# Two tiles' attention blocks side by side on TensorE in a fused window-attention and MoE kernel

## The chip, the cores and the metric

One NeuronCore of a Trainium2 chip runs the whole kernel as one program. The metric is the time of one execution on the device, in microseconds (us); lower is better. The engines are PE (TensorE, matmuls), PEld (its weight loads), DVE (VectorE), ACT (ScalarE), POOL (GpSimd) and SP (SyncE, which here issues the DMAs).

## What is computed

Window attention over q, k and v (8 batches, 8 heads, 576 positions, head width 64, window 64), then a feed-forward block over the 4608 tokens of width 512: hidden width 1024, a softmax-weighted activation, a layer norm with gain, and an output product.

```python
scores = scale * q @ k.T                       # per head
scores = where(0 <= i - j < 64, scores, -1e9)
attn = softmax(scores);  x = attn @ v          # x: 4608 x 512
h = x @ w_in                                   # 4608 x 1024
solu = h * softmax(h)
ln = (solu - mean) / sqrt(var + 1e-6) * g
y = ln @ w_out                                 # 4608 x 512, float32
```

## The kernel before

The tokens are cut into 36 tiles of 128. Iteration t of the main loop emits, in this order on PE: one tiny matmul for the scale of tile t+1 (`x_scale`); the input product of tile t (`moe_in`, 24 matmuls of 128x128 by 128x512 in f16, three passes for accuracy); the values block of tile t+1 (`values`, 32 matmuls of 128x64 in f32, attention weights times v); the scores block of a tile three or four ahead (`scores` inside `attend`, 32 matmuls of 64x64 in f32); and the output product of tile t-3 (`moe_out`, 24 f16 matmuls). Tiles 0 to 2 use f32 products, and the first eight tiles transpose their attention weights on PE (`transposes`); later tiles write them to DRAM and read them back transposed by DMA (`soft_turn`, lines 646 and 649). The layer-norm result goes the same way (`turn`, lines 819 and 822).

The order is made by a small planner, `Plan`. Every operation is registered with an engine, an estimated cost, and what it reads and writes. On PE the planner keeps the order in which the operations were registered. On DVE, ACT, POOL and SP it runs a list schedule: each time an engine is free, the ready operation with the earliest due time is put next, due times being counted back from PE's work. At run time each engine takes its own list strictly in turn.

Buffers are rings, sized in `RINGS`. The ones that matter here lie in PSUM, 8 banks in all: `pH` (hidden layer, two banks, one place), `pS` (scores, two banks, one place), `t` (two places of one bank: early transposes, the scale matmuls, the last tiles' transposes), `pX` (values) and `pO` (output product), one bank each. In SBUF: `qk` 3 places, `v` 4, `vx` 2, `sS` (softmax) 3, `xH` 2, `raw` 4 (first the raw weights, then attention weights and their transposes).

After the scores, `softmax` runs on DVE (line 593 scales and masks, line 598 takes the maximum), ACT (line 602, eight exponentials) and POOL (line 618, scaling), and `soft_planes` (line 638) splits the halves for the DMA. For tiles in `MASKED` PE adds the mask instead (line 549), DVE reduces straight from PSUM in two halves (line 586) and ACT reads PSUM. After the values, ACT (line 708) and DVE (line 709) scale the result into `xH`. After the input product, `moe_norm` reads `pH` three times: maximum on DVE (line 752), exponential on ACT (line 758), product and sum on DVE (line 761); then the layer norm follows. `planes` makes the f16 halves (lines 810 and 813), `join` gathers the values of two blocks (line 532), and line 887 moves the output product out of `pO`. `HOMES` lists, for the first 13 tiles, tasks that run on another engine than their default.

Of the kernel before, what the change touches and what calls it, by code (L numbers as in the profile page):

```python
# [37 lines left out]

HASTE = 1
# [11 lines left out]
    ("PT", 1, 1): "DVE", ("PT", 2, 0): "DVE", ("PT", 4, 0): "DVE", ("PT", 4, 1): "ACT", ("PT", 5, 1): "ACT",  # L51
    ("PT", 6, 0): "DVE", ("PT", 6, 1): "ACT", ("PT", 7, 0): "DVE", ("high", 0, 0): "POOL", ("high", 1, 0): "DVE",
    ("high", 1, 1): "POOL", ("high", 3, 0): "POOL", ("high", 4, 0): "DVE", ("high", 4, 1): "POOL",
    ("high", 5, 0): "POOL", ("high", 5, 1): "POOL", ("high", 6, 0): "POOL", ("high", 7, 0): "POOL",
    ("high planes", 1, 1): "DVE", ("high planes", 2, 0): "POOL", ("high planes", 2, 1): "POOL",
    ("high planes", 3, 0): "DVE", ("high planes", 3, 1): "DVE", ("high planes", 4, 0): "POOL",
    ("high planes", 4, 1): "POOL", ("high planes", 5, 1): "DVE", ("high planes", 6, 0): "DVE",
    ("high planes", 6, 1): "DVE", ("high planes", 7, 0): "POOL", ("high planes", 7, 1): "DVE",
    ("high planes", 8, 0): "POOL", ("high planes", 8, 1): "DVE", ("high planes", 9, 1): "DVE",
    ("high planes", 10, 0): "POOL", ("high planes", 10, 1): "POOL", ("high planes", 11, 0): "POOL",  # L60
    ("high planes", 11, 1): "POOL", ("join", 0, 1): "ACT", ("join", 1, 0): "DVE", ("join", 1, 1): "DVE",
    ("join", 3, 0): "DVE", ("join", 3, 1): "ACT", ("join", 4, 0): "ACT", ("join", 5, 0): "ACT",
    ("join", 7, 0): "ACT", ("join", 8, 0): "DVE", ("join", 10, 0): "DVE", ("join", 10, 1): "POOL",
    ("join", 11, 1): "DVE", ("join", 12, 0): "DVE", ("join", 12, 1): "DVE", ("low bits", 1, 0): "DVE",
    ("low bits", 4, 0): "DVE", ("norm", 4, 1): "DVE", ("norm", 6, 1): "DVE", ("norm", 7, 1): "DVE",
    ("norm", 8, 1): "DVE", ("norm", 9, 0): "DVE", ("norm", 10, 0): "DVE", ("norm", 10, 1): "DVE",
    ("norm", 11, 0): "DVE", ("norm", 12, 0): "DVE", ("norm", 12, 1): "DVE", ("planes", 3, 0): "POOL",
    ("planes", 4, 0): "POOL", ("planes", 5, 1): "POOL", ("planes", 6, 0): "POOL", ("planes", 6, 1): "POOL",
    ("planes", 7, 1): "POOL", ("planes", 8, 0): "POOL", ("planes", 9, 0): "POOL", ("planes", 9, 1): "POOL",
    ("planes", 10, 1): "POOL", ("planes", 11, 1): "POOL", ("planes", 12, 0): "POOL", ("planes", 12, 1): "POOL",  # L70
    ("scale", 0, 0): "ACT", ("scale", 0, 1): "POOL", ("scale", 1, 0): "ACT", ("scale", 1, 1): "POOL",
    ("scale", 2, 0): "ACT", ("scale", 5, 1): "ACT", ("scale", 8, 1): "DVE", ("scale", 9, 1): "ACT",
    ("scale", 11, 0): "ACT", ("scale", 11, 1): "ACT", ("scale", 12, 1): "DVE", ("soft", 8, 0): "DVE",
    ("soft", 8, 1): "ACT", ("soft", 9, 1): "ACT", ("soft", 10, 0): "DVE", ("soft", 10, 1): "ACT",
    ("soft", 11, 0): "DVE",
# [3 lines left out]
MASKED = (1, 4, 5)  # L79
# [145 lines left out]
def tile_window_attention_solu_moe(  # L225
# [312 lines left out]
    def PS(t):  # L538
        return T("pS", t, [P, 2, NPAIR, P], pool=ps_s)

    def scores(t):
        first = first_of(t)

        def emit():
            q, k = Q(t), K(t)
            if t in MASKED:
                mk = masksB[first]
                for r in range(2):
                    nc.tensor.matmul(
                        PS(t)[:, r], identB,  # L550
                        bass.AP(tensor=mk.tensor, offset=mk.offset, ap=[mk.ap[0], [0, NPAIR], mk.ap[1]]),
                        start=True, stop=False)
            for p in range(NPAIR):
                for half in range(2):
                    for r in range(2):
                        rs = slice(r * D, (r + 1) * D)
                        keys = k[rs, p, :P]
                        if half or first == 0:
# [7 lines left out]
                            PS(t)[half * WIN:(half + 1) * WIN, r, p],  # L566
                            q[rs, p, half * WIN:(half + 1) * WIN], keys, start=t not in MASKED,
                            stop=t not in MASKED or p == NPAIR - 1)

        plan.op("PE", 1430 if t in MASKED else 1000, emit, [("qk", t)], [("pS", t)], loose=t < LOOSE)  # L570

    def softmax(t):
# [4 lines left out]
        if t < HEADS:  # L577
            for h in range(H):
                plan.op("DVE", 370, lambda h=h: nc.vector.tensor_tensor_reduce(
                    SS(t)[:, h], PS(t)[:, h // NPAIR, h % NPAIR], mk, scale=-SCALE, scalar=BIG,  # L580
                    op0=ALU.add, op1=ALU.min, accum_out=cols("nmx", h)),
                    [("pS", t)], [("sS", t, h), ("nmx", t, h)], lat=200)
        elif t in MASKED:
            for r in range(2):
                hs = slice(r * NPAIR, (r + 1) * NPAIR)
                plan.op("DVE", 650, lambda r=r, hs=hs: nc.vector.tensor_reduce(
                    T("nmx", t, [P, H], pool=st)[:, hs], PS(t)[:, r], axis=AX.X, op=ALU.max, negate=True),
# [4 lines left out]
        else:  # L592
            plan.op("DVE", 1230, lambda: nc.vector.scalar_tensor_tensor(  # L593
                SS(t), PS(t).rearrange("q r p n -> q (r p) n"), SCALE,
                bass.AP(tensor=mk.tensor, offset=mk.offset, ap=[mk.ap[0], [0, H], mk.ap[1]]),
                ALU.mult, ALU.add),
                [("pS", t)], [("sS", t, h) for h in range(H)])
# [3 lines left out]
        for h in range(H):  # L601
            plan.op("ACT", 580, lambda h=h: nc.scalar.activation(  # L602
                SS(t)[:, h], PS(t)[:, h // NPAIR, h % NPAIR] if t in MASKED else SS(t)[:, h], AF.Exp,
# [75 lines left out]

    def PX(t):  # L680
        return T("pX", t, [P, NC, P], pool=ps_x)
# [9 lines left out]
    def values(t):  # L691
        def emit():
            for p in range(NPAIR):
# [8 lines left out]
        plan.op("PE", 1100, emit, turned(t)  # L702
                + [("v", t), ("vx", t, 0), ("vx", t, 1)], [("pX", t)],
# [151 lines left out]
    def moe_out(t):  # L855
# [3 lines left out]
        def PO():  # L859
            if last:  # L860
                return T(*bank, [P, NC, P], pool=ps_x).rearrange("p a b -> p (a b)")
# [177 lines left out]
```

## Time and profile before

| what | us |
|---|---|
| median of 3 runs | 508.1 |
| the three runs | 506.03, 509.09, 508.1 |
| the profiled execution | 508.81 |
| its span, first to last instruction | 506.6 |
| PE busy in the span | 492.7 |
| DVE, ACT, POOL busy | 391.7, 334.8, 277.5 |

Busy times are unions of the instructions' times on an engine. Matmuls overlap in the array, so a PE that is always busy still loses time where starts are further apart than within a run of equal matmuls. The granted clock of TensorE was 0.999 of full over the span. Idle time of an engine that nobody waits for costs nothing.

### The profile page before, as it was taken

The numbers are of one execution on the slowest core, as the hardware profiler recorded it, in microseconds if no ns is written. First come the engines' busy times: TensorE is split into PE (matmuls) and PEld (weight loads), VectorE is DVE, ScalarE is ACT, GpSimd is POOL, SyncE is SP. The second block draws the span as 40 slices with busy tenths as digits, with TensorE's granted clock in tenths as the row PEclk, the third lists the DMA queues.
The fourth block names the chain that finished last, engine by engine and source line by source line (L and its number), as shares of the span: only waits on it lengthen the run. The fifth ranks groups of instructions, "written<-read, shape, count | busy, mean of one in ns | idle before, by whom it ended". The sixth has DMA issues, their size and how long they took to land.

```text
span 506.6 us, 11800 instructions
## 1 busy us (share of the span) xinstructions
PE 492.7 (97%) x4297; PEld 265.0 (52%) x4297; DVE 391.7 (77%) x875; ACT 334.8 (66%) x958; POOL 277.5 (55%) x477
## 2 busy tenths in 40 slices
PE   8899999999999999999999999999999999999997
PEld 7665555545445555555555555555455555544453
DVE  3798899988898887777887887887787888855430
ACT  5677776678675665767776776776676776764340
POOL 5716768756545666565555555555555556572110
PEclk9999999999999999999999999999999999999999
DMA  8991324769999999999999999999999998778311
GB/s 344 416 390 39 113 74 130 205 180 228 268 249 273 282 240 261 257 270 243 258 269 295 222 277 280 246 272 222 278 252 246 287 251 203 198 234 188 105 41 43
DMA packets 157450, 115.60 MB, mean 228 GB/s; under 512 B 129872, under 2 KB 130128, under 8 KB 156880
## 3 DMA queue, kind: packets, MB, share of 16 engines
q1 hardware_dynamic: 157392, 114.84, 82.3%
q8 instruction: 34, 0.56, 0.5%
q14 instruction: 24, 0.20, 0.1%
HBM read 41.42 MB, written 41.42 MB: 164 GB/s over the span
## 4 chain that ended last, share of the span: by engine, by line
PE 70%; DMA 9%; DVE 5%; SPq 4%; POOL 3%; ACT 1%; issue 1%; ACTq 0%
PE pO L876 29%; PE pH L737 26%; PE pX L698 6%; PE pS L565 5%; DMA raw<-pd 4%; DMA yT<-yd 3%; SPq L822 2%; PE pH L725 1%; SPq L649 1%; PE pX L876 1%; DMA yd<-pl 1%; POOL w_outH L500 1%; DVE raw L378 1%; DVE mst L752 1%; DVE e L761 1%
## 5 line engine op out<-in xcount | busy, mean ns | idle before, releaser
L876 PE MATMUL pO<-w_outH,yT 128*128 128x512 f16 x544 | 167.7, 380 | 2.7 <-DMA yT<-yd 2.5
L737 PE MATMUL pH<-w_inH,xH 128*128 128x512 f16 x528 | 161.8, 379 | 0.3 <-DVE xH L709 0.3
L618 POOL TENSOR_SCALAR sS<-sS,rec 128x128 f32<-128x128 f32 x252 | 102.4, 425 | 79.3 <-DVE rec L614 60.8
L876 PEld LDWEIGHTS <-yT 128*128 128x128 f16 x840 | 79.6, 98 | 99.6 <-issue 4.7
L737 PEld LDWEIGHTS <-xH 128*128 128x128 f16 x792 | 75.1, 98 | 89.2 <-DVE xH L709 0.8
L602 ACT ACTIVATE sS<-sS,nmx 128x128 f32<-128x128 f32 x264 | 102.3, 391 | 16.5 <-DVE nmx L598 11.1
L876 PE MATMUL pO<-w_outL,yT 128*128 128x512 f16 x272 | 103.1, 379 | 0.0
L737 PE MATMUL pH<-w_inL,xH 128*128 128x512 f16 x264 | 99.0, 379 | 0.0
L782 POOL TENSOR_SCALAR e<-e,mst 128x512 f32<-128x512 f32 x62 | 50.8, 826 | 50.3 <-DVE mst L756 31.6
L752 DVE TENSOR_REDUCE mst<-pH 128x1 f32<-128x1024 f32 x36 | 44.0, 1223 | 34.4 <-PE pH L737 33.3
L887 ACT ACTIVATE ot<-pO,bound 128x512 f32<-128x512 f32 x34 | 23.3, 685 | 57.6 <-PE t_x L469 48.3
L708 ACT ACTIVATE xH<-pX,xscale 128x512 f16<-128x512 f32 x33 | 22.7, 687 | 43.9 <-PE pX L698 43.6
L776 POOL TENSOR_TENSOR mst<-mst,neghalf 128x1 f32<-128x1 f32 x36 | 20.3, 564 | 56.1 <-DVE mst L774 53.4
L638 POOL COPY raw<-sS 128x1024 uint16<-128x1024 uint16 x50 | 50.7, 1040 | 0.2
L602 ACT ACTIVATION_READ_ACCUMULATOR sS<-sS,nmx 128x1 f32 x264 | 50.1, 190 | 0.0
L769 ACT ACTIVATE unread<-e,mst 128x1024 bf16<-128x1024 f32 x36 | 41.0, 1139 | 12.6 <-DVE mst L764 11.2
L758 ACT ACTIVATE e<-pH,mst,xscale 128x1024 f32<-128x1024 f32 x33 | 39.6, 1199 | 11.0 <-DVE mst L756 11.0
L761 DVE CUSTOM_DVE_ANT_0 e<-pH,e 128x1024 f32<-128x1024 f32 x36 | 43.7, 1215 | 2.7 <-ACT e L758 2.6
L813 DVE TENSOR_TENSOR pl<-e,pl 128x512 f16<-128x512 f32 x49 | 39.5, 809 | 2.0 <-ACT pl L810 1.9
L565 PE MATMUL pS<-qk 64*64 64x128 f32 x1152 | 40.6, 280 | 0.0
L598 DVE TENSOR_REDUCE nmx<-sS 128x8 f32<-128x1024 f32 x32 | 38.5, 1202 | 0.0
L593 DVE SCALAR_TENSOR_TENSOR sS<-pS,maskNone 128x1024 f32<-128x1024 f32 x26 | 31.6, 1216 | 3.8 <-PE pS L565 3.7
(131 smaller groups left out, 714.9 us busy)
## 6 DMA issues: line engine op xcount, KB each, us to landing
qk<-qk SPq DMA_DIRECT2D x36, 640.0 KB, 5.1
yd<-pl SPq DMA_DIRECT2D x33, 512.0 KB, 3.4
pd<-raw SPq DMA_DIRECT2D x28, 512.0 KB, 4.0
v<-vS SPq DMA_DIRECT2D x36, 256.0 KB, 3.5
y<-ot SPq DMA_DIRECT2D x35, 256.0 KB, 3.4
raw<-w_in SPq DMA_DIRECT2D x4, 1024.0 KB, 10.6
raw<-w_out SPq DMA_DIRECT2D x4, 1024.0 KB, 9.9
yT<-yd SPq DMA_TRANSPOSE x33, 5.1
```

The costliest lines, as they stand in the source:

```text
L565: nc.tensor.matmul(PS(t)[half * WIN:(half + 1) * WIN, r, p], q[rs, p, half * WIN:(half + 1) * WIN], keys, start=t not in MASKED, stop=t no ...
L602: plan.op("ACT", 580, lambda h=h: nc.scalar.activation(SS(t)[:, h], PS(t)[:, h // NPAIR, h % NPAIR] if t in MASKED else SS(t)[:, h], AF.Ex ...
L618: SS(t)[:, h], SS(t)[:, h], rec()[:, h:h + 1]) if e == "ACT" else units[e].tensor_scalar(
L638: plan.op(e, {"POOL": 1050, "ACT": 1000, "DVE": 700}[e], lambda x=x, e=e: copy_on(e)(PP(t)[:, :, 4 * x:4 * x + 4].rearrange("p k h n -> p ...
L737: plan.op("PE", 218, lambda n=n, c=c, k=k, w=w: nc.tensor.matmul(PH(t)[:, hs], X(t, k)[:, c], w(c, h), start=(n == 0), stop=(n == len(pass ...
L752: plan.op("DVE", 1230, lambda: nc.vector.tensor_reduce(nmax(), PH(t), axis=AX.X, op=ALU.max, negate=True), [("pH", t)], [key(0)])
L758: plan.op("ACT", 1320, lambda: nc.scalar.activation(E(t), PH(t), AF.Exp, bias=nmax(), scale=XS(t, 2) if scaled else 1.0, accum_out=se()), ...
L761: plan.op("DVE", 1310, lambda: nc.vector.tensor_tensor_reduce(E(t), PH(t), E(t), scale=1.0, scalar=0.0, op0=ALU.mult, op1=ALU.add, accum_o ...
L769: plan.op("ACT", 1330, lambda: nc.scalar.activation(unread, E(t), AF.Square, bias=nmean(), scale=1.0, accum_out=ss()), H2 + [key(4)], [key ...
L782: plan.op(e, {"POOL": 820, "DVE": 600}[e], lambda h=h, hs=hs, e=e: units[e].tensor_scalar(E(t)[:, hs], E(t)[:, hs], nmean(), kk(), ALU.add ...
L813: plan.op(e, {"POOL": 1160, "DVE": 920}[e], lambda hs=hs, e=e: units[e].tensor_sub(PL(t)[:, 1, hs], E(t)[:, hs], PL(t)[:, 0, hs]), [("e", ...
L876: plan.op("PE", 216, lambda f=f, i=i, x=x, k=k, y=y, w=w: nc.tensor.matmul(PO(), Y(t, y)[:, f], w(i, x), start=(f == k == 0), stop=(f == N ...
```

## The change

Constants: `PAIRS = 13` and `WIDER = (7,)` are new, tile 1 leaves `MASKED`, and `HOMES` is another list of 93 entries (80 tasks of the first 13 tiles move to another engine or back to their default).

In odd iterations t = 13, 15, ... 29 (`begins(t)`) the loop registers the scale matmuls, joins and values of tiles t+1 and t+2 and then the scores of tiles t+5 and t+6, one after the other, all between the input product of t and the output product of t-3. In the iteration after each, none of these is registered, so that the input product, the output product and the next iteration's scale matmuls follow each other.

The values of t+1 then lie in the bank of `pO`, those of t+2 in `pX`. The scores of t+6 lie in the two places of `t`, one for each half of the heads, and DVE reads them with two passes in place of one.

From iteration 7 on, scores are registered one more tile ahead (iteration 7 registers two tiles' scores). The loads of q and k follow that; the loads of v are registered by themselves. Some cost estimates of the planner differ.

```diff
-MASKED = (1, 4, 5)
+MASKED = (4, 5)
+    def begins(t):
+        return PAIRS <= t < NTILE - 6 and (t - PAIRS) % 2 == 0
+    def aside(t):
+        return begins(t - 6)
+    def PS(t, r):
+        if aside(t):
+            return T("t", f"s{t}{r}", [P, NPAIR, P], pool=ps_t)
+        return T("pS", t, [P, 2, NPAIR, P], pool=ps_s)[:, r]
...
-        plan.op("PE", 1430 if t in MASKED else 1000, emit, [("qk", t)], [("pS", t)], loose=t < LOOSE)
+        plan.op("PE", 1430 if t in MASKED else 870 if t > PAIRS + 4 else 1040, emit, [("qk", t)], list(dict.fromkeys(scored(t))), loose=t < LOOSE)
...
+            n = NPAIR if aside(t) else H
+            for x in range(H // n):
+                hs = slice(x * n, (x + 1) * n)
+                plan.op("DVE", 1230 if n == H else 670, lambda x=x, hs=hs: nc.vector.scalar_tensor_tensor(
+                    SS(t)[:, hs], PS(t, x) if aside(t) else whole(), SCALE,
...
+    def at_X(t):
+        return ("pO", f"x{t}") if begins(t - 1) else ("pX", t)
...
-        plan.op("PE", 1100, emit, turned(t)
-                + [("v", t), ("vx", t, 0), ("vx", t, 1)], [("pX", t)],
+        plan.op("PE", 1030 if begins(t - 2) else 1100 if begins(t - 1) else 1210, emit, turned(t)
+                + [("v", t), ("vx", t, 0), ("vx", t, 1)], [at_X(t)],
...
-            plan.op("PE", 218, lambda n=n, c=c, k=k, w=w: nc.tensor.matmul(
+            plan.op("PE", 216, lambda n=n, c=c, k=k, w=w: nc.tensor.matmul(
...
     def ahead(t):
-        at = t + AHEAD + (t >= FURTHER)
-        return range(at - (t == FURTHER), at + 1)
+        if begins(t) or begins(t - 1):
+            return range(t + 5, t + 7) if begins(t) else range(0)
+        wide = (t >= FURTHER) + sum(t >= x for x in WIDER)
+        at = t + AHEAD + wide
+        return range(at - (t == FURTHER) - (t in WIDER), at + 1)
...
-            on(load, a + 1)
+            on(load, a + 1, (0,))
+        for a in range(t + 4, t + 5 + begins(t)) if not begins(t - 1) else ():
+            on(load, a, (1,))
...
-        on(x_scale, t + 1)
+        paired = begins(t) or begins(t - 1)
+        for a in range(t + 1, t + 3) if begins(t) else () if paired else (t + 1,):
+            on(x_scale, a)
...
-            on(join, t + 1)
-            on(values, t + 1)
-            for a in ahead(t)[:1]:
+            for f in (join, values):
+                for a in range(t + 1, t + 3) if begins(t) else () if paired else (t + 1,):
+                    on(f, a)
+            for a in ahead(t)[:2 if paired else 1]:
                 on(attend, a)
...
-            for a in ahead(t)[1:]:
+            for a in ahead(t)[1:] if not paired else ():
                 on(attend, a)
```

## Rows read from the trace of the kernel before

**Rows 1.** Chain that ended last, in order of time: start us, us, what

```profile
148.08 5.20 PE pH L737 x24
...
231.85 5.29 PE pO L876 x24
...
242.34 1.08 PE pX L698 x32
243.43 1.03 PE pS L565 x32
244.46 5.29 PE pO L876 x24
...
440.10 5.20 PE pH L737 x24
```

**Rows 2.** Busy times by stretch, early and steady: columns in the first line

```profile
core 0: us, PE busy (x) PEld busy (x) DVE busy (x) ACT busy (x) POOL busy (x), PEclk, DMA share, GB/s
60.00:148.00 88.00, 84.14 (x761) 45.99 (x761) 81.89 (x188) 63.91 (x190) 57.35 (x85) 1.00 0.71 188
198.80:300.00 101.20, 100.90 (x905) 52.12 (x904) 81.00 (x176) 72.03 (x208) 57.65 (x105) 1.00 0.99 261
```

**Rows 3.** PE timeline at one values and scores block: start us, us, instruction

```profile
203.77 0.38 PE L737 MATMUL pH<-w_inH,xH 128*128 128x512 f16 x1
...
204.36 0.29 PE L698 MATMUL pX<-raw,vx 128*64 128x64 f32 x4
...
204.95 0.29 PE L698 MATMUL pX<-raw,v 128*64 128x64 f32 x4
205.16 1.10 PE L565 MATMUL pS<-qk 64*64 64x128 f32 x32
```

**Rows 4.** Groups by line: busy us, mean ns | idle before, releaser

```profile
L876 PE MATMUL pO<-w_outH,yT 128*128 128x512 f16 x544 | 167.7, 380 | 2.7 <-DMA yT<-yd 2.5 <-ACT ot L887 0.3
...
L565 PE MATMUL pS<-qk 64*64 64x128 f32 x1152 | 40.6, 280 | 0.0
...
L593 DVE SCALAR_TENSOR_TENSOR sS<-pS,maskNone 128x1024 f32<-128x1024 f32 x26 | 31.6, 1216 | 3.8 <-PE pS L565 3.7
...
L532 DVE COPY vx<-v 64x512 f32<-64x512 f32 x8 | 4.9, 609 | 0.1
L810 DVE CAST pl<-e 128x512 f16<-128x512 f32 x9 | 4.3, 489 | 0.0
```

**Rows 5.** PE timeline at the longest stall of the steady stretch

```profile
356.92 0.34 PE L698 MATMUL pX<-raw,vx 128*64 128x64 f32 x4 [1.11 <-DMA raw<-pd]
```

**Rows 6.** SP timeline, the two transposes of a tile and its longest plain issue

```profile
232.35 3.80 SPq L649 DMA_TRANSPOSE raw<-pd  x1
236.25 3.27 SPq L822 DMA_TRANSPOSE yT<-yd  x1
...
240.94 0.66 SPq L646 DMA_DIRECT2D pd<-raw  x1
```

**Rows 7.** Waits of SP's queue: us in total, times, longest us

```profile
SPq L525 <- PE pX L698: 52.4, 27, 3.3
```

**Rows 8.** DMA issues from 198.8 to 300 us: count, median us to landing

```profile
yT<-yd SPq DMA_TRANSPOSE x8, 6.3
```

**Rows 9.** DVE timeline, passes over pH and beside them in three iterations

```profile
292.81 1.22 DVE L752 TENSOR_REDUCE mst<-pH 128x1 f32<-128x1024 f32 x1 [0.82 <-PE pH L737]
...
294.62 0.75 DVE L709 SCALAR_TENSOR_TENSOR xH<-pX,xscale,xH 128x512 f16<-128x512 f32 x1 [0.34 <-ACT xH L708]
...
296.42 1.22 DVE L761 CUSTOM_DVE_ANT_0 e<-pH,e 128x1024 f32<-128x1024 f32 x1
...
309.37 1.21 DVE L761 CUSTOM_DVE_ANT_0 e<-pH,e 128x1024 f32<-128x1024 f32 x1
...
448.33 1.23 DVE L761 CUSTOM_DVE_ANT_0 e<-pH,e 128x1024 f32<-128x1024 f32 x1 [0.43 <-ACT e L758]
```

**Rows 10.** PE timeline, first matmul of the input product after two of these

```profile
300.04 0.38 PE L737 MATMUL pH<-w_inH,xH 128*128 128x512 f16 x1
...
312.65 0.38 PE L737 MATMUL pH<-w_inH,xH 128*128 128x512 f16 x1
```

More of the change, by code (lines that the diff above doesn't have):

```diff
@@ L37 @@
 FURTHER = 4
+PAIRS = 13
+WIDER = (7,)
 HASTE = 1
@@ L50 @@
 HOMES = {
[L51 to L75, printed above, removed]
+    ("PT", 0, 1): "DVE", ("PT", 1, 1): "DVE", ("PT", 2, 0): "DVE", ("PT", 4, 0): "DVE", ("PT", 4, 1): "ACT",
+    ("PT", 5, 1): "ACT", ("high", 0, 0): "POOL", ("high", 1, 1): "POOL", ("high", 3, 0): "POOL",
@@ new lines @@
+    ("high planes", 10, 0): "DVE", ("high planes", 10, 1): "DVE", ("high planes", 11, 0): "DVE",
+    ("high planes", 12, 0): "POOL", ("high planes", 12, 1): "POOL", ("join", 0, 1): "DVE", ("join", 1, 1): "ACT",
+    ("join", 2, 1): "ACT", ("join", 3, 0): "DVE", ("join", 3, 1): "ACT", ("join", 4, 0): "ACT",
+    ("join", 4, 1): "ACT", ("join", 6, 0): "ACT", ("join", 7, 0): "ACT", ("join", 7, 1): "ACT",
+    ("join", 9, 0): "POOL", ("join", 9, 1): "DVE", ("join", 10, 0): "POOL", ("join", 10, 1): "POOL",
@@ new lines @@
+    ("join", 11, 0): "POOL", ("join", 12, 0): "DVE", ("join", 12, 1): "POOL", ("low bits", 1, 0): "DVE",
+    ("low bits", 4, 0): "DVE", ("norm", 3, 0): "DVE", ("norm", 4, 0): "DVE", ("norm", 6, 0): "DVE",
+    ("norm", 6, 1): "DVE", ("norm", 7, 0): "DVE", ("norm", 7, 1): "DVE", ("norm", 8, 1): "DVE",
+    ("norm", 10, 0): "DVE", ("norm", 12, 0): "DVE", ("norm", 12, 1): "DVE", ("planes", 3, 1): "POOL",
+    ("planes", 4, 0): "POOL", ("planes", 4, 1): "POOL", ("planes", 5, 0): "POOL", ("planes", 5, 1): "POOL",
@@ new lines @@
+    ("planes", 6, 1): "POOL", ("planes", 8, 1): "POOL", ("planes", 9, 1): "POOL", ("planes", 10, 0): "POOL",
+    ("planes", 10, 1): "POOL", ("planes", 11, 0): "POOL", ("planes", 12, 0): "POOL", ("scale", 0, 0): "ACT",
+    ("scale", 0, 1): "POOL", ("scale", 1, 0): "ACT", ("scale", 1, 1): "POOL", ("scale", 2, 0): "ACT",
+    ("scale", 5, 1): "ACT", ("scale", 6, 0): "ACT", ("scale", 8, 1): "ACT", ("scale", 9, 0): "ACT",
+    ("scale", 9, 1): "ACT", ("scale", 10, 1): "ACT", ("scale", 11, 0): "DVE", ("scale", 11, 1): "ACT",
@@ L76 @@
+    ("soft", 6, 0): "DVE", ("soft", 6, 1): "DVE", ("soft", 7, 0): "DVE", ("soft", 8, 1): "ACT",
+    ("soft", 9, 0): "ACT", ("soft", 9, 1): "DVE", ("soft", 11, 0): "DVE", ("soft", 12, 0): "ACT",
 }
 HEADS = 1
-MASKED = (1, 4, 5)
+MASKED = (4, 5)
 SCALES = 2
@@ L592, in softmax, with whole @@
         else:
[L593 to L597, printed above, removed]
+            def whole():
+                return T("pS", t, [P, 2, NPAIR, P], pool=ps_s).rearrange("q r p n -> q (r p) n")
+            n = NPAIR if aside(t) else H
[3 more added lines that the diff above has]
+                    SS(t)[:, hs], PS(t, x) if aside(t) else whole(), SCALE,
+                    bass.AP(tensor=mk.tensor, offset=mk.offset, ap=[mk.ap[0], [0, n], mk.ap[1]]),
+                    ALU.mult, ALU.add),
+                    [scored(t)[x]], [("sS", t, h) for h in range(H)[hs]])
             plan.op("DVE", 1230, lambda: nc.vector.tensor_reduce(
@@ L860, in PO @@
             if last:
[L861 removed]
+                return T(*bank, [P, DM], pool=ps_x)
             return T(*bank, [P, DM], pool=ps_o)
```

27 lines of the change are left out of this document (16 added, 11 removed).

## The prediction

> **What bounds the kernel now.** I read the chain that ended last, in order of time, first, since it says who set the end. From 148 us to 480 us it is almost only PE: in one iteration 24 matmuls for the output product, 24 for the input product, one block of values, one block of scores, and again; 12.61 us from one output product to the next [rows 1]. The busy times by stretch came next: of 101.2 us there PE is busy 100.9, at the full granted clock, DVE 81.0, ACT 72.0, POOL 57.7 [rows 2]. So in this stretch a saving on PE is a saving of time, as long as nothing else becomes late.
>
> Within the 12.61 us, what is not streaming? Before the values a matmul starts every 0.216 us: the 48 f16 ones take 10.37 us, the scale matmul 0.03 us. In the PE timeline the values' groups of four start 0.118 us apart (204.36 to 204.95 in five steps), eight groups 0.94 us. The scores' 32 matmuls start at 205.16 and take 1.10 us to the end of the last, which itself takes 0.28 [rows 4]: the last starts near 205.98, 31 steps in 0.82 us, so 0.85 us in all [rows 3]. 12.61 - 10.37 - 0.03 - 0.94 - 0.85 = 0.42 us is lost at three changes of shape: 128x128 f16 to 128x64 f32, that to 64x64 f32, and back. The first is visible: from the last f16 start (203.77) to the third group (204.36) are 0.59 us, where 0.216 + 2 x 0.118 = 0.45 would do: 0.14 us. The second: 205.16 - 204.95 - 0.118 = 0.09 us, and the slow first step of the scores.
>
> Two other losses. From iteration 9 to 32, 23 periods take 440.10 - 148.08 = 292.02 us; 23 x 12.61 = 290.03, so 2.0 us went to stalls, the longest one 1.11 us of idle before the values of tile 26, which waited for the transposed softmax [rows 1, 5]. Before 148 us PE idles too: the 2.5 us that the output product waited for transposed activations [rows 4] fall there, and DVE is busy 81.9 of 88.0 us [rows 2]: a stage with other limits.
>
> **The change, part by part.** *Pairs.* In nine iterations (13, 15, ... 29) PE does two values blocks and then two scores blocks; in the nine between, none. The three shape changes are paid once for two tiles. If the second block of a kind pays nothing, that is 9 x 0.42 = 3.8 us. No row of before has two values or two scores blocks back to back. The lower end: the second values block pays the 0.09 us start of a new kind and the second scores block as much, 0.18 us a pair, leaving 9 x 0.24 = 2.2 us; the upper end is 3.8. I take 3.8: within a block the groups already alternate between operands and PSUM columns at an even 0.118 us [rows 3], and a second block differs only in that. The Trainium skill's page TensorEngine Tiling (Array Packing), section Key Properties, says that TensorE drains when the tiling mode changes and not when only the tile does; by it the second block pays nothing and the sum takes 3.8, by the lower end above it would be 2.2. That the 0.42 us lie at changes of mode agrees with it; that a second block is free no run here shows yet.
>
> *Scores one tile earlier* (WIDER, at iteration 7; two ahead in pairs). A tile's scores now stand four iterations before its values, not three: about 12.6 us more for softmax, its write and its DMA transpose. Stalls of the kind in [rows 5] should go: -2.0 us. Its DMAs move with it. SP has per tile two transposes (3.80 and 3.27 us of issue) and five plain issues, the longest 0.66 us [rows 6], at most 10.4 of 12.6 us; a pair needs the same in 25 us, but its two value loads both stand in the queue until the two values blocks free the places. Already now SP waits at those loads for the values, 52.4 us over 27 tiles [rows 7], and behind it are the transposes. A transpose of activations issued at 236.25 lands in the median 6.3 us later [rows 6, 8], at 242.6, for the output product at 244.46 [rows 1]: 1.9 us to spare at this, an early and tight, place. I count nothing for it and keep up to 0.4 us in each of nine pairs (3.6 us) as the bad end.
>
> *The input product after an empty iteration.* The hidden layer has one PSUM place: the next input product waits until DVE's product pass (line 761) has read it. Now values, scores and output product cover that pass; in the nine odd iterations only the output product does, 2.21 us less (12.61 - 10.37 - 0.03). What is spare today: the pass ends at 297.64 and the next input product starts at 300.04, 2.40 us [rows 9, 10]; in the next iteration it ends at 310.58 and the start is 312.65, 2.07 us. Left as they are, these give +0.19 and -0.14 us. But the scaling pass (line 709, 0.75 us) that stands before line 761 in both is not there in an odd iteration, and where DVE has nothing between, it waits 0.43 us for ACT and starts at once (the last of [rows 9]). Against that, two tiles' softmax passes (1.22 us each [rows 4]) are queued on DVE since the even iteration, and one may be in the way. Best: no stall. Worst: -0.14 and one pass of 1.2 us, 1.3 us. I take 0.1 us, nearest to the two rows: 9 x 0.1 = +0.9 us.
>
> *Values in the output bank.* The first values block of a pair takes the output product's bank, so that product waits until ACT and DVE have scaled it. In [rows 9] line 709 ends at 295.37, about 1.5 us after the values (input product read from 292.81, values 1.08 us [rows 1]). The cover is the second values block and two scores blocks, 0.94 + 2 x 0.85 and two changes of shape: 2.8 us. Hidden with 1.3 us to spare; bare it would cost up to 1.5 us a pair. The scores in the two small banks are read by two DVE passes for one; bound from zero to one more 1.22 us pass, nearest to a split of it with a little overhead: 9 x 0.1 us, on a DVE with 20 of 101 us free [rows 2]. Nothing.
>
> *Homes, and tile 1 without the PE mask.* Up to tile 12, counted task by task, DVE gets four casts (0.49 us) and four joins (0.61) fewer [rows 4], 4.4 us, besides smaller swaps; ACT gets more of it. Against that tile 12's scores come earlier, two passes of 1.22 us, and tile 1 takes the wide pass instead of two half ones, under 1.2 us more. DVE ends level or lighter. At best the 2.5 us of idle before 148 us goes; at worst the extra tile's DVE work shows in full and a little more, +3. PE's mask matmuls of tile 1 stand among filler matmuls, worth nothing. I take -0.5 us. The altered costs in the plan (218 to 216 and others) only shape the order.
>
> Sum, against the profiled execution's 508.8 us (span 506.6): 508.8 - 3.8 - 2.0 + 0.9 - 0.5 = **503.4 us**. That execution lies 0.7 us above the median of 508.1; stalls that differ from run to run can make that much, and they are taken out here, so I do not shift the sum. It is 0.9% under the median.
>
> **The rivals.** A: *the input product becomes the wait* (ends slower). If a 1.2 us pass stands before line 752 or 761 in each odd iteration, the stall is 1.3 us: 503.4 - 0.9 + 11.7 = 514.2. It cancels the pairs' 3.8 us and the 2.0 from 0.64 us each, and makes the kernel 1% slower from about 1.2 us. For it: two tiles' softmax in one iteration. Against: DVE was idle until PE ended before most of today's reductions, so low-priority passes ran out. Chance 0.06; a smaller form, 0.5 us each, 507.0: 0.11.
>
> B: *DMA issue takes the gain back*: 0.4 us in each pair for a late transpose, 503.4 + 3.6 = 507.0. For it: DMA share 0.99 in the steady stretch [rows 2] and little spare above. Against: PE barely waited there, and the softmax side gains 12.6 us. Chance 0.10; in its full form, an SP list that never rests and holds the period at 12.61 us whatever PE does, only the early 0.5 us stays, about 508 (0.02 of the 0.10): SP's at most 10.4 of 12.6 us speak against it. The Trainium skill, Perfetto Trace Analysis, section What "DMA-bound" means, names this case, the DMA sequencer, and its sign is a track of solid DMA slices; SP's is not solid here.
>
> C: *the early stage moves by itself*: idle gone, 501.4 (0.18), or softmax not hidden, +3, 506.9 (0.09). For the first: DVE, the busiest engine there, gets lighter; for the second: it had only 6 us free and takes on a tile earlier.
>
> D: *the second block pays again*: 3.8 becomes 2.2, 505.0. For it: no row has two blocks in a row; against: the even steps inside a block. Chance 0.06.
>
> **How the numbers follow.** The forecast has the rest, 0.40. The range reaches from 499.5, where C's better side comes with no stall in the odd iterations and a little more, to 508.5, past B, C's worse side and the smaller A; it leaves out A in full and the places where two of these meet. A measurement of this kernel can tell about 1% from no change, 5.1 us: 503.0 and 513.2 are the bounds. The forecast lies at the first, so half its share counts as faster, 0.20, with C's better side 0.18 and some of D and of the smaller cases gone well, 0.04: 0.42 in all; slower 0.07, A in full and a meeting of B with C; within 1% the rest, 0.51.
>
> **What would show it.** Pairs: two iterations together about 24.8 us, not 25.2; a second values block 0.94 us after the first, a second scores block 0.85 us. Stalls: no idle before values. Odd iterations: line 761 ending before the next input product; if PE's input product waits for line 761, A. If the output product waits for transposes after 200 us, B. If the time at which iteration 13 starts moves from 198.8 us by more than 2 us, C. I am wrong if the pair period isn't shorter or iteration 13 starts late.

## The result, and the profile after

The changed kernel takes 501.24 us (median; 500.78 to 501.54), the kernel before 508.39 us beside it (506.03 to 509.09). The ratio is 0.9867, with a 95% interval of 0.983 to 0.990: 1.3% faster, where 503.4 us, 0.9% under, was forecast. It lies inside the range, on the far side of C's better end. The profiled execution is 501.21 us, its span 499.4 us; both kernels run at a granted clock of 1.0 in the stretches compared.

The busy times of the page come first, then the group of the output product that answers to [rows 4], with a DVE group of which the prediction did not speak. The columns of a group are busy us, mean ns, and the idle time of the engine before it with what ended most of it.

```profile
PE 487.3 (98%) x4297; PEld 264.4 (53%) x4297; DVE 376.4 (75%) x869; ACT 343.3 (69%) x976; POOL 279.1 (56%) x472
```

```profile
L902 PE MATMUL pO<-w_outH,yT 128*128 128x512 f16 x544 | 167.6, 380 | 1.6 <-DVE xH L735 1.2 <-ACT ot L913 0.3 <-DMA yT<-yd 0.2
...
L798 DVE SCALAR_TENSOR_TENSOR mst<-mst 128x1 f32<-128x1 f32 x36 | 16.4, 455 | 6.9 <-ACT unread L795 6.7
```

PE's wait for transposed activations fell from 2.5 us [rows 4] to 0.2; a new one of 1.2 us, for DVE at line 735, has come. The input product starts (line 737 before, 763 after) cut the span into stretches:

| iteration starts at (us) | 3 | 9 | 13 | 31 | end |
|---|---|---|---|---|---|
| before | 59.89 | 147.94 | 198.81 | 427.35 | 506.63 |
| after | 58.41 | 144.72 | 196.75 | 421.25 | 499.44 |

By stretch, up to iteration 3, then 3 to 9, 9 to 13, 13 to 31 and to the end, the change makes -1.5, -1.7, +1.2, -4.0 and -1.1 us. The last term is a block of scores that is now done before iteration 9.

The windows of the early and of the paired stage (columns as in [rows 2]):

```profile
58.40:144.70 86.30, 85.27 (x792) 46.77 (x792) 78.38 (x182) 69.47 (x212) 55.77 (x75) 1.00 0.75 198
...
196.75:421.25 224.50, 223.34 (x2037) 117.53 (x2036) 175.68 (x407) 162.79 (x470) 128.60 (x232) 1.00 1.03 262
```

In the early one DVE has 78.4 us of work where 81.9 stood, and ACT 69.5 for 63.9 [rows 2].

The chain that ended last, in order of time, over a pair and at the place of the new wait:

```profile
196.89 5.20 PE pH L763 x24
202.09 1.08 PE pO_x L724 x32
203.18 0.93 PE pX L724 x32
204.11 1.03 PE pS L582 x32
205.14 0.87 PE t_s L582 x32
206.02 5.29 PE pO L902 x24
211.30 5.18 PE pH L763 x24
216.48 5.18 PE pO L902 x24
221.69 5.20 PE pH L763 x24
...
251.73 1.22 DVE mst L778
252.95 2.15 DVE mst L798
...
255.29 0.67 DVE xH L735
```

By `begins(t)` an iteration with the pair is odd (13, 15, ... 29) and takes 14.39 us; the one after it is even, has neither values nor scores and takes 10.41 us. Below they are called full and empty. The prediction, where it speaks of the input product and its wait, and the recorded expectations that name the two call the empty ones odd and the full ones even; what they say of the work in them is right, the parity is the other way round.

The pair is plain PE work: from 196.89 to 221.69 are 24.80 us, the number forecast, where two iterations of [rows 1] take 25.22. The second values block is 0.15 us shorter than the first, the second scores block 0.16 us. In three of the nine pairs (iterations 17, 19 and 23) the chain leaves PE for DVE, as at 251.73, and the full iteration takes 14.83 us instead of 14.39.

PE's timeline shows the changes of block and the two waits:

```profile
189.39 0.34 PE L724 MATMUL pX<-raw,vx 128*64 128x64 f32 x4 [1.50 <-DMA raw<-pd]
...
202.89 0.29 PE L724 MATMUL pO_x<-raw,v 128*64 128x64 f32 x4
203.00 0.29 PE L724 MATMUL pX<-raw,vx 128*64 128x64 f32 x4
...
204.04 1.10 PE L582 MATMUL pS<-qk 64*64 64x128 f32 x32
204.96 1.05 PE L582 MATMUL t_s<-qk 64*64 64x128 f32 x32
...
221.55 0.38 PE L763 MATMUL pH<-w_inH,xH 128*128 128x512 f16 x1
...
256.00 0.38 PE L902 MATMUL pO<-w_outH,yT 128*128 128x512 f16 x1 [0.38 <-DVE xH L735]
```

Into the second values block the step is 0.11 us (202.89 to 203.00), as between groups of one block. The Trainium skill's page TensorEngine Tiling (Array Packing), section Key Properties, says that TensorE drains when the tiling mode changes and not when only the tile does; this step, between two blocks of one mode, agrees. The first row is a wait of 1.50 us for the transposed softmax before the values of tile 13. They stand in iteration 12, alone, as the last values block before the first pair; it is called the entry wait below. Such waits should have gone.

DVE's timeline, in an empty iteration (14) and in one of the three disturbed full ones (17):

```profile
219.42 1.22 DVE L787 CUSTOM_DVE_ANT_0 e<-pH,e 128x1024 f32<-128x1024 f32 x1 [1.11 <-ACT e L784]
...
251.73 1.22 DVE L778 TENSOR_REDUCE mst<-pH 128x1 f32<-128x1024 f32 x1 [1.57 <-PE pH L763]
252.87 2.23 DVE L798 SCALAR_TENSOR_TENSOR mst<-mst 128x1 f32<-128x1 f32 x1
...
255.21 0.74 DVE L735 SCALAR_TENSOR_TENSOR xH<-pO_x,xscale,xH 128x512 f16<-128x512 f32 x1
```

The product pass (line 787) ends at 220.64; the next input product starts at 221.55, 0.91 us later, without a wait. In the disturbed pair line 798, one number per partition, takes 2.23 us, and line 735, which frees the output bank, is late by it. POOL's timeline at that place:

```profile
253.07 2.02 POOL L661 COPY raw<-sS 128x1024 uint16<-128x1024 uint16 x2
```

Line 798 ends at 255.10, and the two copies at 255.09.

### The profile page after: what moved, and what is told of

Same layout as the page of the kernel before. It is cut to its first block, busy times and chain, and to the rows that moved or that the text cites. A ratio compares the mean times of both kernels' runs of the same rounds, so it can differ in the third digit from the quotient of the medians.

```text
span 499.4 us, 11779 instructions
## 1 busy us (share of the span) xinstructions
PE 487.3 (98%) x4297; PEld 264.4 (53%) x4297; DVE 376.4 (75%) x869; ACT 343.3 (69%) x976; POOL 279.1 (56%) x472
## 4 chain that ended last, share of the span: by engine, by line
PE 78%; DVE 7%; DMA 6%; POOL 4%; ACT 3%; issue 1%; SPq 1%; ACTq 0%
PE pO L902 33%; PE pH L763 30%; PE pX L724 4%; PE pS L582 4%; PE pH L751 3%; DMA raw<-w_in 2%; DMA raw<-pd 2%; DMA yT<-yd 2%; DVE mst L778 1%; DVE mst L798 1%; PE pO_x L724 1%; ACT w L375 1%; POOL sS L641 1%; POOL w_outH L503 1%; PE t_s L582 1%; PE pX L902 1%
## 5 line engine op out<-in xcount | busy, mean ns | idle before, releaser
L902 PEld LDWEIGHTS <-yT 128*128 128x128 f16 x840 | 80.6, 98 | 98.8 <-issue 4.4
L641 POOL TENSOR_SCALAR sS<-sS,rec 128x128 f32<-128x128 f32 x244 | 98.8, 424 | 41.7 <-DVE rec L637 11.1
L625 ACT ACTIVATE sS<-sS,nmx 128x128 f32<-128x128 f32 x272 | 105.3, 390 | 6.6 <-DVE nmx L596 4.5
L802 POOL TENSOR_TENSOR mst<-mst,neghalf 128x1 f32<-128x1 f32 x36 | 21.5, 597 | 81.6 <-DVE mst L800 79.5
L625 ACT ACTIVATION_READ_ACCUMULATOR sS<-sS,nmx 128x1 f32 x272 | 51.6, 190 | 0.0
L839 DVE TENSOR_TENSOR pl<-e,pl 128x512 f16<-128x512 f32 x50 | 40.8, 827 | 3.7 <-ACT pl L836 3.6
L836 ACT CAST pl<-e 128x512 f16<-128x512 f32 x51 | 30.0, 614 | 14.8 <-POOL e L808 12.7
L621 DVE TENSOR_REDUCE nmx<-sS 128x8 f32<-128x1024 f32 x33 | 39.8, 1206 | 0.0
L535 ACT COPY vx<-v 64x512 f32<-64x512 f32 x57 | 35.0, 615 | 0.6
L582 PE MATMUL pS<-qk 64*64 64x128 f32 x864 | 29.9, 276 | 0.2 <-DMA qk<-qk 0.2
```

The lines of the kernel that those rows point to most:

```text
L582: nc.tensor.matmul(PS(t, r)[half * WIN:(half + 1) * WIN, p], q[rs, p, half * WIN:(half + 1) * WIN], keys, start=t not in MASKED, stop=t no ...
L621: plan.op("DVE", 1230, lambda: nc.vector.tensor_reduce(T("nmx", t, [P, H], pool=st), SS(t), axis=AX.X, op=ALU.max, negate=True), [("sS", t ...
L625: plan.op("ACT", 580, lambda h=h: nc.scalar.activation(SS(t)[:, h], PS(t, h // NPAIR)[:, h % NPAIR] if t in MASKED else SS(t)[:, h], AF.Ex ...
L641: SS(t)[:, h], SS(t)[:, h], rec()[:, h:h + 1]) if e == "ACT" else units[e].tensor_scalar(
L839: plan.op(e, {"POOL": 1160, "DVE": 920}[e], lambda hs=hs, e=e: units[e].tensor_sub(PL(t)[:, 1, hs], E(t)[:, hs], PL(t)[:, 0, hs]), [("e", ...
L902: plan.op("PE", 216, lambda f=f, i=i, x=x, k=k, y=y, w=w: nc.tensor.matmul(PO(), Y(t, y)[:, f], w(i, x), start=(f == k == 0), stop=(f == N ...
```

## The experiments

Three questions stand behind the number. What are the pairs, the earlier scores and the homes worth apart? Are the input products after empty iterations and the shared banks as safe as assumed? And what holds line 798? Ratios are to the kernel before, with 95% intervals.

**No pairs.** `begins` is never true; scores stand one tile earlier and the homes are new.

```diff
-PAIRS = 13
+PAIRS = 99
```

> The changed kernel without pairs (PAIRS beyond the last tile): scores one tile earlier, new homes and tile 1 without the mask stay. Theory (each pair saves one set of three shape changes): every steady period is 12.61 us again, so nine pairs give back 9 x 0.41 = 3.7 us; the three 0.44 us waits of the output product for the values in its bank go (-1.3 us), and the changed kernel's 501.2 us becomes about 503.6. Rival (what was won came from earlier scores and the early stage alone): 500 to 501.5 us, with periods that are paid for elsewhere.

Measured: 502.0 us (501.93 to 502.43), ratio 0.9867 [0.983, 0.990]. Two windows, iterations 3 to 9 and 13 to 31:

```profile
58.45:144.70 86.25, 85.34 (x793) 46.84 (x793) 78.55 (x182) 69.49 (x212) 55.79 (x75) 1.00 0.75 199
195.10:422.00 226.90, 226.90 (x2036) 117.22 (x2035) 172.56 (x395) 161.29 (x466) 133.19 (x239) 1.00 1.01 258
```

Eighteen periods take 226.90 us, 12.61 each with no stall: the pairs are not needed to end them. The pairs' 224.50 are 2.4 us less: nine times 0.41, less three waits of 0.44. But iteration 13 starts at 195.10 here and at 196.75 after, since the entry wait is missing here. That was not expected (503.6 was). Net, 3.7 - 1.3 - 1.6 leaves 0.8 us for the pairs, as the medians do; the ratios are equal, and the difference is not clear of noise.

**The homes of before**, the rest as changed.

```diff
 HOMES = {
-    ("PT", 0, 1): "DVE", ("PT", 1, 1): "DVE", ...
+    ("PT", 1, 1): "DVE", ("PT", 2, 0): "DVE", ...
```

> The changed kernel with the HOMES of before. Theory (the new homes made the early stage shorter): iteration 3's input product starts near 59.9 us again instead of 58.4 and iteration 13's by 2 to 3 us later than 196.75; the median goes to about 503.5 to 504.5. Rival (tile 1's mask off PE made it shorter, or the earlier scores): iteration 3 starts at 58.4 as now, the median stays within 1 us of 501.2.

Measured: 504.77 us (503.13 to 506.9), ratio 0.9929 [0.989, 0.997]; iteration 13 starts at 201.06, not 196.75. So the new homes are worth 3.5 us by the medians, where 0.5 was taken. The profiled execution is one of the longer ones (506.57); of its 5.3 us over after, 4.3 lie ahead of iteration 13. There PE waits 2.3 us for transposed softmax in three iterations between 9 and 13, against 1.5 us in after. In iteration 14 a wait of rival A's kind takes 0.9 us, and iteration 3 starts at 59.25, nearer to before than to after.

**Scores earlier, alone**: homes of before and no pairs.

```diff
-PAIRS = 13
+PAIRS = 99
 HOMES = {
-    ("PT", 0, 1): "DVE", ("PT", 1, 1): "DVE", ...
+    ("PT", 1, 1): "DVE", ("PT", 2, 0): "DVE", ...
```

> Scores one tile earlier from iteration 7, with the HOMES of before and without pairs. Theory (the effects add: earlier scores take away the steady stalls, homes shorten the early stage, pairs save 0.41 us each less their own waits): iterations 13 to 31 take 226.9 us as without pairs, iteration 13 starts near 200 us, the median is 505.5. Rival (the new homes only make good what the earlier scores cost in the early stage): iteration 13 starts near 198.8 us and the median is 503.5 or less.

Measured: 506.08 us (504.27 to 507.65), ratio 0.9953 [0.993, 0.997]. The same two windows:

```profile
58.70:146.80 88.10, 86.43 (x800) 47.48 (x798) 83.21 (x191) 62.82 (x192) 57.68 (x86) 1.00 0.71 197
197.75:424.90 227.15, 227.09 (x2037) 117.25 (x2036) 173.53 (x396) 164.02 (x468) 126.41 (x226) 1.00 1.02 256
```

Earlier scores take the steady stalls away by themselves (227.15 against 228.54 before, 12.62 a period). Iteration 13 starts at 197.75, where the theory had 200 and the rival 198.8, while the median is near the theory's; its profiled execution (504.9) is one of the shorter ones. By the ratios the effects add within noise: 0.5% for the earlier scores, 0.9% for the homes on top of them, nothing for the pairs on top of both. What this run has over before is more than the earlier scores: tile 1 without the mask, the altered cost estimates and the loads of v registered by themselves came with them, and of these only the mask was tried apart. Old homes leave 88.10 us for the early stage and DVE 83.2 us of work in it; with the new ones (no pairs, above) it is 86.25 and 78.6, while ACT goes from 62.8 to 69.5. Work went from a DVE with 5 us free in that stage to an ACT with 25 free.

**Tile 1's scores masked on PE again.**

```diff
-MASKED = (4, 5)
+MASKED = (1, 4, 5)
```

> The changed kernel with tile 1 masked on PE again (two half passes on DVE instead of the wide pass and the reduction). Theory (the homes made the early stage shorter, not this): iteration 3's input product starts within 0.5 us of 58.4 and the median within 0.6 us of 501.2. Rival (this made it shorter): iteration 3 starts near 59.9, the median near 502.7.

Measured: 502.33 us (500.0 to 502.54), ratio 0.9861 [0.982, 0.990]: no effect to be seen. Iteration 3 starts at 58.50, after at 58.41. Its profiled execution (500.0) is the shortest of four; the others took 502.1 to 502.5. Among the profiled executions with the new homes that start lies anywhere from 58.38 to 59.29, and at 58.70 with earlier scores alone and old homes, so it is not known how much of the 1.5 us at the start belongs to the change, nor that any of it is the homes'.

**One tensor less for line 798**: the same product by a form with one tensor and two per-partition scalars.

```diff
-        plan.op("DVE", 130, lambda: nc.vector.scalar_tensor_tensor(
-            kk(), se(), se(), ss(), ALU.mult, ALU.mult), [key(1), key(3)], [key(5)])
+        plan.op("DVE", 130, lambda: nc.vector.tensor_scalar(
+            kk(), ss(), se(), se(), ALU.mult, ALU.mult), [key(1), key(3)], [key(5)])
```

> The changed kernel with one small DVE instruction per tile written otherwise: se*se*ss as one tensor with two per-partition scalars instead of two tensors and a scalar (line 798); the same plan and order. Theory (that instruction, 128x1 with two tensors in SBUF, cannot go on while POOL's copies at line 661 run: 2.23 us in three iterations, ending with the copy, and the output product then waits 0.44 us): no instance over 0.4 us, the three pairs of 25.24 us become 24.80, the median falls by about 1.3 us to 499.9. Rival (it waits for something else, or the scalars are read in the same way): the long instances stay, 501.2.

Measured: 500.9 us (500.45 to 502.85), ratio 0.9851 [0.981, 0.989]. The group, then DVE's and POOL's timelines at one meeting of the two:

```profile
L798 DVE TENSOR_SCALAR mst<-mst 128x1 f32<-128x1 f32 x36 | 9.5, 265 | 6.8 <-ACT unread L795 6.7
```

```profile
252.11 0.27 DVE L798 TENSOR_SCALAR mst<-mst 128x1 f32<-128x1 f32 x1
...
344.36 0.69 DVE L458 TENSOR_REDUCE vmost<-v 128x1 bf16<-128x512 f32 x1 [3.13 <-DMA v<-vS]
345.28 1.17 DVE L787 CUSTOM_DVE_ANT_0 e<-pH,e 128x1024 f32<-128x1024 f32 x1
```

```profile
252.31 2.02 POOL L661 COPY raw<-sS 128x1024 uint16<-128x1024 uint16 x2
```

All 36 take about 0.27 us, also right beside a copy, and all nine full iterations take 14.39 us: the 0.44 us waits came from that operand form. The median lies 0.3 us under that of after, where 1.3 was forecast, and inside the noise. At the end of iteration 24, an empty one, PE's timeline has a wait that after has not:

```profile
346.52 0.39 PE L763 MATMUL pH<-w_inH,xH 128*128 128x512 f16 x1 [1.59 <-DVE mst L787]
```

This is rival A, once: line 787 stood on DVE behind line 458, which waited 3.13 us for a load of v. It cost 1.6 us, more than the 1.3 us that the edit frees; the entry wait was 0.90 us in this execution.

**A longer chain in empty iterations**: one more pass over the hidden layer after line 787, whose result nobody uses.

```diff
+        if begins(t - 1):
+            plan.op("DVE", 1230, lambda: nc.vector.tensor_reduce(
+                col(6), PH(t), axis=AX.X, op=ALU.max, negate=True), [("pH", t), key(2)], [key(6)])
```

> The changed kernel with one pass more on DVE over the hidden layer (128x1024, result unused) behind line 787 in the nine odd iterations, so that the hidden layer is given back 1.1 to 1.2 us later. In the changed kernel that pass ends 0.91 us before the next input product starts in an undisturbed odd iteration. Theory (the cover of an odd iteration is nearly used up, this wait is next): a stall of 1.15 - 0.91 + about 0.1 = 0.3 us in each odd iteration, 9 x 0.3 = 2.7 us, about 504. Rival (there is more room than the spare time shows, or DVE absorbs it): 501.2, odd periods stay 10.41 us.

Measured: 518.4 us (515.66 to 520.08), ratio 1.019 [1.012, 1.026]. DVE's timeline at one empty iteration, and PE's waits (us in total, times, longest us):

```profile
247.54 0.88 DVE L842 TENSOR_TENSOR pl<-e,pl 128x512 f16<-128x512 f32 x1
248.34 1.21 DVE L791 TENSOR_REDUCE mst<-pH 128x1 f32<-128x1024 f32 x1
```

```profile
PE pH L763 <- DVE mst L791: 12.3, 8, 2.1
```

Eight empty iterations now wait for the added pass, 12.3 us in all, and the ninth waits 1.5 us for an operation queued behind it. So DVE's passes over the hidden layer are what stands next in an empty iteration, and the cover is about as thin as the 0.91 us read from after. The size was mis-forecast (504): in eight of the nine a planes pass (line 842) also slipped in ahead of the added one, so that the hidden layer came back 1.9 us later at this place, not 1.15.

**The banks the other way round**: the first values block goes to the values' bank, the second, with less work behind it, to the output bank.

```diff
-        return ("pO", f"x{t}") if begins(t - 1) else ("pX", t)
+        return ("pO", f"x{t}") if begins(t - 2) else ("pX", t)
...
-        ... pool=ps_o if begins(t - 1) else ps_x ...
+        ... pool=ps_o if begins(t - 2) else ps_x ...
```

> The changed kernel with the two banks of a pair's values exchanged: the first block in the values' bank, the second in the output product's. Theory (the output product waits for the scaling of whatever lies in its bank, and only the first block's is done in time): the second block's scaling pass ends 0.5 to 2.2 us after the output product could start, so even iterations take 14.9 to 16.6 us instead of 14.39, 5 to 20 us in all, 506 to 521. Rival (the wait is hidden behind the scores either way): even iterations 14.4 us, 501.2.

Measured: 511.15 us (510.59 to 513.86), ratio 1.006 [1.004, 1.009]. PE's waits (us in total, times, longest us):

```profile
PE pO L902 <- DVE xH L735: 9.8, 8, 1.2
```

Eight of the nine full iterations take 15.66 us, 1.27 more. The order of the banks alone turns the change into a loss: as changed, the scaling is covered by a values block and two scores blocks, here by the scores alone. The profiled execution is the longest of the ten (513.86); its entry wait is 2.09 us.

**Scores one per iteration**, values still in pairs.

```diff
-            for a in ahead(t)[:2 if paired else 1]:
+            for a in (t + 5,) if paired else ahead(t)[:1]:
```

> The changed kernel with the values still in pairs but one scores block in each iteration. Theory (a block between f16 products pays its changes of shape each time): an odd iteration gains one scores block with its own changes, 0.87 + 0.17 = 1.04 us, an even one loses 0.87 only, so two iterations take 24.97 us instead of 24.80, 9 x 0.17 = 1.5 us, about 502.7; the odd iteration's input product has about 1 us more cover. Rival (the saving is all at the values): 24.80 us, 501.2.

Measured: 502.47 us (two executions, 502.33 and 502.62), ratio 0.987 [0.981, 0.994]. The chain:

```profile
204.38 1.03 PE pS L582 x32
205.41 5.29 PE pO L902 x24
210.70 5.18 PE pH L763 x24
215.88 1.03 PE t_s L582 x32
216.91 5.29 PE pO L902 x24
```

The pair takes 13.51 + 11.55 = 25.06 us, 0.26 more than after and 0.16 less than before. A lone block of scores starts and ends with a change of shape: 1.03 us and an output product of 5.29, against 0.87 for the second in a row and 5.18 for an output product that follows f16 work. That splits the saving of 0.41 us: 0.16 from values in pairs, about 0.26 from scores.

**Pairs with as little else as possible**: homes and masks of before, scores moved only at iteration 12.

```diff
-WIDER = (7,)
+WIDER = (12,)
 HOMES = {
-    ("PT", 0, 1): "DVE", ("PT", 1, 1): "DVE", ...
+    ("PT", 1, 1): "DVE", ("PT", 2, 0): "DVE", ...
-MASKED = (4, 5)
+MASKED = (1, 4, 5)
```

> The kernel before with the pairs alone: its HOMES and its mask on tile 1 are kept, and scores go one tile further ahead at iteration 12 only, right before the pairs, not at 7. Theory (pairs and earlier scores shorten the steady stretch whatever the early stage does): iterations 13 to 31 take 223 to 225 us instead of 228.5, iteration 13 starts near 200 us, and the median is 503.5 to 505. Rival (the pairs pay only with the new early stage, since the backlog of transposes at the entry decides): a stall of over 1.5 us at the entry or in the pairs, 506 to 508.

Measured: 514.84 us (512.95 to 516.86), ratio 1.012 [1.006, 1.017]. PE's timeline at its longest wait:

```profile
214.94 0.48 PE L725 MATMUL pX<-raw,vx 128*64 128x64 f32 x4 [9.43 <-DMA raw<-pd]
```

The forecast was ten us too low: tile 15's scores stood only two iterations ahead of its values, so PE waited 9.43 us for softmax and its transpose. That iteration took 12.2 us more than an undisturbed full one. The other 2.8 us come with a lower clock: PE did next to nothing for 9.4 us, and from 215 to 219 us its granted clock was 0.50, the lower of its two levels (1.2 GHz). Of the eight pairs after that four are as short as in after (24.80 us), and four wait 0.55 us for line 736, the scaling pass that is 735 in after, and take 25.40. Scores one tile earlier are not an extra beside the pairs but what lets them start.

**A fifth place for v**, with line 798 mended, against the late load that held line 787.

```diff
-    "raw": 4, "w": 8, "qk": 3, "v": 4, ...
+    "raw": 4, "w": 8, "qk": 3, "v": 5, ...
```

> The changed kernel with the small DVE instruction at line 798 written with one tensor and two scalars, and with five places for the value tiles instead of four. Theory (in an odd iteration whatever DVE waits for ahead of line 787 delays the input product; in the run with the first edit alone that was once the largest-value pass of line 458, 3.1 us idle for a late value load): with five places the loads come earlier, no input product waits for line 787, all pairs take 24.80 us, iterations 13 to 31 take 223.2 us; with the stall at the entry (iteration 12, 1.0 to 1.6 us) left, the median is 499.5. Rival (earlier loads crowd the transposes in SP's queue): new waits for the transposes, 501 or more.

Measured: 502.14 us (500.72 to 504.26), ratio 0.988 [0.983, 0.993]. Behind iteration 13 the pairs take 24.80 us, but for one that still waits 0.15 us for line 787. But iteration 7 takes 14.6 us, 0.8 more than in after, and in iteration 13 PE waits for activations:

```profile
207.67 0.39 PE L902 MATMUL pO<-w_outH,yT 128*128 128x512 f16 x1 [1.70 <-DMA yT<-yd]
```

What was won later is lost there. **Pairs from tile 11**, and **from tile 9**, both on top of the last:

```diff
-PAIRS = 13
+PAIRS = 11
```

> As f1, with pairs from iteration 11: ten pairs. Theory: one pair more saves 0.41 us, and the stall at the entry comes at another iteration with about the same size: 499.1. Rival (the entry sits where the softmax transposes have least room, 0.1 to 1.3 us of spare time in iterations 9 to 12, and a pair needs two of them at once): the values of the first pair wait 2 us or more, 501.

> As f1, with pairs from iteration 9: eleven pairs. Theory: two pairs more save 0.8 us, 498.7. Rival (as for pairs from 11, but nearer to iteration 7, where two tiles' scores were added): the first pair's second block waits 3 us or more for its transposed weights, 502.

Measured: 504.63 us (501.8 to 505.43), ratio 0.991 [0.988, 0.995], and 506.71 us (502.4 to 508.47), ratio 0.997 [0.993, 1.000]. PE's timeline of the first, then DVE's and PE's of the second:

```profile
179.84 0.48 PE L724 MATMUL pX<-raw,vx 128*64 128x64 f32 x4 [3.43 <-DMA raw<-pd]
```

```profile
223.97 0.69 DVE L458 TENSOR_REDUCE vmost<-v 128x1 bf16<-128x512 f32 x1 [3.23 <-DMA v<-vS]
```

```profile
225.92 0.39 PE L763 MATMUL pH<-w_inH,xH 128*128 128x512 f16 x1 [1.56 <-DVE mst L787]
```

The first pair comes too early for its softmax in both: iteration 11 takes 19.57 us in the one, iteration 9 17.01 in the other, where 14.4 was hoped for. In the first the granted clock was 0.50 from 180 to 183 us, behind the wait of 3.43 us, so the iteration lost more than the wait. From tile 9 there are also six waits of the input product for line 787, 5.9 us together. In four of them line 458 stands in front, waiting for v as in iteration 24 above, so five places for v did not prevent them; in the first, at the end of iteration 8, two softmax passes stand there.

No version here is clearly faster than the changed kernel; the one with line 798 mended lies within its interval.

## Why the prediction was right or wrong

**Pairs, -3.8: right.** The saving is 0.41 us a pair, 3.7 in all, the second block is free, and rival D (505.0) is out.

**Values in the output bank, "nothing": wrong in three of nine pairs**, 1.3 us together. The cover was counted rightly: in six pairs it held, and the experiment with the banks swapped shows that without the second values block 1.27 us a pair are lost. What failed is the duration of what it covers: about 1.5 us was taken from one undisturbed place in [rows 9], with line 798 at its short length. The longer case was to be read in the trace of before, in a group not among the rows:

```profile
L772 DVE SCALAR_TENSOR_TENSOR mst<-mst 128x1 f32<-128x1 f32 x36 | 17.4, 484 | 10.2 <-ACT unread L769 10.1
```

A mean of 484 ns for one number per partition, with 0.6 to 2.2 us in 9 of 36 iterations, is a wait in disguise. In before it had cover enough.

**Stalls of the steady stage, -2.0: right in mechanism and size.** Without pairs, and with the new homes, none is left from iteration 9 to 31. Between 13 and 31 that is 228.54 - 18 x 12.61 = 1.6 us, and 0.4 us lie between 9 and 13.

**The entry, which no step foresaw, +1.6.** The wait for the transposed softmax returns once, before the values of tile 13, one iteration ahead of the first pair. SP's timeline ahead of it in after, then without pairs, where PE did not wait:

```profile
171.50 2.17 SPq L848 DMA_TRANSPOSE yT<-yd  x1
...
180.76 0.42 SPq L669 DMA_DIRECT2D pd<-raw  x1
181.28 5.93 SPq L672 DMA_TRANSPOSE raw<-pd  x1
```

```profile
180.52 4.50 SPq L672 DMA_TRANSPOSE raw<-pd  x1
185.11 0.53 SPq L669 DMA_DIRECT2D pd<-raw  x1
```

Rival B looked for late transposes in every pair; the late one stands before the first pair. The profiles of the eight kernels with pairs from 13, or none, and the new homes fall into two groups. In five the write of tile 14's softmax (line 669) stands ahead of the transpose of tile 13 in SP's list, which takes its entries strictly in turn: after, one tensor, longer chain, banks the other way round, scores one per iteration. There the transpose starts at 180.6 to 182.0 us, takes 5.8 to 6.0 us to issue, and PE waits 0.90 to 2.09 us. In three the write stands behind it: no pairs, tile 1's mask, a fifth place for v. There the transpose starts at 178.9 to 180.5 us, takes 4.4 to 4.5 us, and PE does not wait for it. So the wait goes with the order that the planner gave to SP, and pairs do not need that order: tile 1's mask has the pairs and not the wait. No run changed this order alone, and **what sets the length of a transpose's issue stays open**: the one of tile 12 took 5.62 us in after with the next write behind it. Two of the three without this wait had waited 0.83 and 0.77 us for the same kind of transpose earlier, in iteration 7.

**The input product after an empty iteration, +0.9: mis-sized.** In after none of the nine loses time. The rows taken had a scaling pass ahead of line 761; without it the chain from the end of the input product to the end of line 787 is at its shortest, 4.3 us, and 0.91 us is spare. Rival A's mechanism is real all the same: one added pass brings it out for 12.3 us, and a DVE pass waiting for a late v brings it out for 1.6 us in iteration 24. What would make it decide was named as softmax passes in the way; in iteration 24, and in most such waits of the other runs, it was line 458 waiting for a DMA.

**The early stage, -0.5: the term that missed most.** Stretches up to iteration 9 gained 3.2 us while doing one scores block more, 1.1 us that come back at the end: 4.3 us. By the experiments the new homes are worth most of that (3.5 and 4.1 us by the medians, over the whole kernel). Direction and reason, a lighter DVE, stood in the prediction as C's better side, at 501.4 us and a chance of 0.18. The failed step was the bound: "at best the 2.5 us" counted only what the output product waited for. The whole idle of PE in that stage was 88.0 - 84.1 = 3.9 us [rows 2], and in after 86.3 - 85.3 = 1.0 us is left of it; what was gained ahead of iteration 3 lay outside the bound altogether, and its part is uncertain, as said above. Tile 1 without the mask did nothing, as assumed.

**Together**: -3.7 - 2.0 + 1.3 + 1.6 - 4.3 makes -7.1 us against the span's -7.2. The total came out near because two misses against it (2.9 us) met two in its favour (0.9 and 3.8). So the forecast was near partly by luck. By the ratios about half a per cent is the earlier scores', 0.6 to 0.9 the homes', and what the pairs bring net, 0 to 1.3 us by ratios and medians, these runs can't tell from nothing: their 3.7 us are there in the periods and are lost again to line 798 and at the entry.

## What to carry to other kernels

Changes of operand shape on a full PE are worth counting, but a gain of 0.41 us a pair lives only as long as every engine behind it keeps its cover: to empty one iteration of two took 2.2 us of cover from it here, and a first pair whose scores stood too few iterations ahead cost more than all pairs gained. Where the busiest engine behind PE is at 93% in a stage (DVE, 81.9 of 88.0 us), look for gains in moving work off it, and bound them by the whole idle time of the engine that sets the end, not by its one largest wait. Look at a group whose mean is far above its shortest instances, and at a DVE pass that waits for a load: both hold up the work queued behind them.

## What was not expected of the hardware

A DVE operation on one number per partition, with two tensors from SBUF, took 2.23 us (mean 0.455 us over 36) and ended with two POOL copies, 0.01 us after them; with one tensor and two per-partition scalars it takes 0.27 us beside the same copies. All nine instances over 0.4 us in after, and all nine over 0.5 us in before, end within 0.02 us of the end of a POOL operation. The Trainium skill's page SBUF — State Buffer, section "SBUF: two separate sides", says that a DVE operation with two SBUF inputs and a GpSimd operation that reads SBUF lock each other out for a whole instruction; the trace agrees, by these numbers.

A DMA transpose took SP 2.17 us (activations) and 5.93 us (softmax) to issue within 16 us of one execution, where the two read ahead of the prediction took 3.80 and 3.27 [rows 6]; so a sum over SP's queue from one pair of rows was no bound.

An idle PE can cost more than its idle time: the granted clock was 0.50 for some microseconds behind idle stretches of 3.43 us (pairs from tile 11) and 9.43 us (pairs with as little else as possible), and stayed at 1.00 behind those of 1.50 us (after) and 1.70 us (a fifth place for v).
